# Global units' scores and values in the four accumulator banks at the start of a chunk

## The chip, the cores and the metric

One Trainium2 chip, one of its cores. The kernel is timed as a whole, in microseconds on the device; a figure for a kernel is the median of several runs. Five engines work side by side, each through its own queue in order: TensorE (PE; PEld is its weight load), VectorE (DVE), ScalarE (ACT), GpSimd (POOL) and SyncE (SP), which issues the DMA transfers. They wait for each other by semaphores.

## The reference

Attention with a window and a few global tokens, then a feed-forward layer with a norm ahead of it and a residual sum. Batch 8, 8 heads, 512 local and 32 global tokens, head dimension 64, so a model width of 512 and a hidden width of 2048.

```
s_g = scale * matmul(q_g, concat(k_g, k_l)^T)              # global queries see all 544 keys
out_g = matmul(softmax(s_g), concat(v_g, v_l))
s_ll = where(|i - j| <= 32, scale * matmul(q_l, k_l^T), -1e9)
out_l = matmul(softmax(concat(scale * matmul(q_l, k_g^T), s_ll)), concat(v_g, v_l))
x = concat(out_g, out_l) per token, heads side by side
out = x + relu((x - mean) / sqrt(var + 1e-6) * g_ln @ w_ch1) @ w_ch2
```

## The kernel before

**Chunks.** The local tokens are 16 halves of 256 tokens; two halves are a chunk of 512, chunks 0 to 7, and the 256 global tokens are the last, chunk 8. For each chunk `Ffn.run` goes through f = 0 to 15, 128 hidden units each. hidden(f) is 12 matmuls (line 777) into one of the two banks of `ps_h`. relu(f), on ScalarE, writes `hh` (line 788), rest(f), on VectorE, writes `hl` (line 792); both read that bank, and with rest(f) it comes free. out(f) is 4 times 3 matmuls (line 804) into the four accumulators `acc` of `ps_o`; the first of the three takes `hl`. On TensorE stand hidden(0), hidden(1), out(0), hidden(2), out(1) and so on. After out(15) line 836 adds the residual, held in tile `ob`, to each accumulator, and line 837 stores it. So the accumulators hold nothing from that sum to out(0) of the next chunk.

**What runs in between.** During chunk c the attention of chunk c+1 is made, piece by piece. `step()` is called three times in each hidden(f), once ahead of each of the four parts of out(f), and runs the next piece of a generator from the queue `first` or else `side`. At place 2f or 2f+1 (ahead of hidden(f) or behind it) `stage` adds generators to `side`. All engines' orders are as written (manual schedule).

A **pair** (`Pair`, four per chunk, places 1, 8, 16, 23) is two heads' pairs of a half: scores into two banks of `ps_a` (line 436), two reductions of four parts (line 454), exponentials (line 469), transposes by 32x32 blocks on VectorE (`turn_blocks`, line 395), values (line 504) into a bank of `ps_h`, sums on POOL, output (lines 521, 523). `attend(u, before, last)` runs pair u's scores, the earlier pair's values, half of u's reductions, the output of the earlier pair, the other half. Every second pair ends a half: its tokens are then normalized (lines 226 to 242, with a power on POOL between lines 228 and 236) and turned, also by line 395.

A **global unit** (`Global`, eight: one each in chunks 1 to 6, two in chunk 7) holds the 32 global queries of four batches and two heads. Its scores are 544 columns, made as two parts of 272, each into both banks of `ps_a`, from `ride` at places 3 and 6 through the queue `first`; reductions are line 582, exponentials line 595, transposes at places 11 and 16, values (line 627) at the end of the pair at place 23. `load`, called there for the next unit, asks for queries, keys and values together. The last two units run in chunk 7.

**Banks of `ps_h`.** A pair's values take the bank that is free when TensorE comes to them. For the pair at place 16, whose values stand between out(6) with hidden(7) behind it and hidden(8), that is the bank of f=6, and hidden(8) then takes the bank of f=7: it needs rest(7).

Of the kernel before, what the change touches and what calls it, by code (L numbers as in the profile page):

```python
# [83 lines left out]
def attention_ffn_kernel(  # L84
# [457 lines left out]
    class Global:  # L542


        def __init__(self, bg, hp):
            self.at = bg, hp
            self.next = None
            self.pt = None

        def load(self):  # L550
            ap = apool
            self.q = ap.tile([P, BG, SG], F32, name="gq", tag="gq")
            self.k = ap.tile([P, BG, SA], F32, name="gk", tag="gk")
            self.v = [wtmp.tile([P, BG, 2, P], F32, name="gv", tag="tmp", bufs=2) for _ in range(2)]
            self.vt = const.tile([P, P], F32, name="gvt", tag="band")
            nc.sync.dma_start(self.q, gq[self.at])
            nc.sync.dma_start(self.k, gk[self.at])
# [4 lines left out]
        def scores(self, part):  # L562
            if part == 0:
                self.p = apool.tile([P, 2, SA], F32, name="gp", tag="gp")
                self.mn = small.tile([P, 4], F32, name="gmn", tag="mn2")
                self.sm = small.tile([P, 2], F32, name="gsm", tag="sm2")
            p, mn = self.p, self.mn
            c0, c1 = part * SA // 2, (part + 1) * SA // 2
            sc = [ps_a.tile([P, 512], F32, name="sc", tag="att") for _ in range(2)]
            for i in range(BG):  # L570
                for h in range(2):
                    nc.tensor.matmul(  # L572
                        sc[h][i * SG:(i + 1) * SG, :c1 - c0],
                        self.q[h * D:(h + 1) * D, i, :],
                        self.k[h * D:(h + 1) * D, i, c0:c1],
                        start=True,
                        stop=True,
                        tile_position=(h * D, i * SG),
                        skip_group_check=True,
                    )  # L580
            for h in range(2):
                nc.vector.tensor_scalar(
                    p[:, h, c0:c1],
                    sc[h][:, :c1 - c0],
                    -QSCALE,
                    BIG if part == 0 else mn[:, 2 * h:2 * h + 1],
                    ALU.mult,
                    ALU.min,
                    accum_out=mn[:, 2 * h + part:2 * h + part + 1],
                )  # L590
            yield
            if part == 0:
                return
            for h in range(2):
                nc.scalar.activation(
                    p[:, h, :],
                    p[:, h, :],
                    AF.Exp,
                    bias=mn[:, 2 * h + 1:2 * h + 2],
                    scale=-1.0,  # L600
                    accum_out=self.sm[:, h:h + 1],
                )
                yield

        def turned(self):
            if self.pt is None:
                pt = apool.tile([P, 2, SA], F32, name="gpt", tag="gk")
                self.pt = pt[:, :, :4 * P].rearrange("p h (c q) -> p h c q", c=4)
                self.tail = pt[:, :, 4 * P:]
# [9 lines left out]

        def values(self):  # L620
            bg, hp = self.at
            pv = ps_a.tile([P, 512], F32, name="pv", tag="att")
            for h, c in [(h, c) for h in range(2) for c in range(4)] + [(0, 4), (1, 4)]:
                hd = slice(h * D, (h + 1) * D)
                for i in range(BG):
# [9 lines left out]
                    )  # L635
            ri = small.tile([P, 2], F32, name="gri", tag="ri2")
            nc.gpsimd.tensor_scalar(ri, self.sm, SUM_EPS, None, ALU.add)
            yield
            nc.vector.reciprocal(ri, ri)
            x = apool.tile([P, P], F32, name="gx", tag="gq")  # L640
            nc.vector.tensor_tensor(
                x.rearrange("p (h d) -> p h d", h=2),
                pv[:, :P].rearrange("p (h d) -> p h d", h=2),
                ri.unsqueeze(2).to_broadcast([P, 2, D]),
                op=ALU.mult,
            )
            to = xs.rearrange("(b s) d -> b s d", b=B)[bg * BG:(bg + 1) * BG, :SG]
            nc.sync.dma_start(to[:, :, hp * P:(hp + 1) * P], x)
            if self.next:
                self.next.load()  # L650
            yield

# [225 lines left out]

    def attend(u, before, last):

        if u:
            u.scores()
            if u.next:
                u.next.load_scores()
        if before:
            before.values()
            before.sums()
            if before.next:
                before.next.load_values()
# [36 lines left out]
        for n in range(4 if u else 0):  # L926
            u.turn(4 + n)
            yield

    xt = []  # L930
# [105 lines left out]
    for token in pend:  # L1036
        firsts.does(token)
    side.append(finish_first())
    new = list(zip(pairs[5:] + [None], pairs[4:]))
    for c, chunk in enumerate(chunks):  # L1040
        if c == 1:
            globals_[0].load()
        if chunk is None:
# [10 lines left out]

        def ride(u, places):
            for n, place in enumerate(places[:2]):
                put(place, lambda n=n: first.append(u.scores(n)) or ())
            for n, place in enumerate(places[2:]):
                put(place, lambda n=n: u.turns(n))

        if 0 < c < last_chunk - 1:
            for place in PAIR_PLACES:
                u, before = new.pop(0)
                last = globals_[c - 1].values if place == PAIR_PLACES[-1] else None
                put(place, lambda u=u, before=before, last=last: attend(u, before, last))
            ride(globals_[c - 1], (3, 6, 11, 16))
        if c == last_chunk - 1:
            ready[last_chunk] = [new_x()]
            x = ready[last_chunk][0]
            put(2, lambda: load_global_tokens(0))  # L1070
            ride(globals_[c - 1], (1, 4, 6, 8))
            put(11, globals_[c - 1].values)
            ride(globals_[c], (14, 16, 17, 18))
            put(21, globals_[c].values)
            put(22, lambda: load_global_tokens(1))
# [109 lines left out]
```

## Time and profile before

| | |
|---|---|
| median of 3 runs (lowest, highest) | 908.58 us (907.88, 909.33) |
| span of the profiled execution | 904.6 us |
| TensorE busy | 886.3 us (98%) |
| VectorE busy | 647.9 us (72%) |
| ScalarE busy | 306.6 us (34%) |
| GpSimd busy | 36.2 us (4%) |
| mean granted TensorE clock | 0.994 |

A row of time gives start, length, engine, line of the program, operation, tile written and read, shape, count of instructions merged into it; in brackets stands the idle time of the engine before it and who ended it. A matmul of 32-bit floats that is not rounded (line 436, 504, 572, 627) leaves two records. Records of matmuls overlap, since they are pipelined: the start of the next tells more than an end.

### The profile page before, as it was taken

The numbers are of one execution on the slowest core, as the hardware profiler recorded it, in microseconds if no ns is written. First come the engines' busy times: TensorE is split into PE (matmuls) and PEld (weight loads), VectorE is DVE, ScalarE is ACT, GpSimd is POOL, SyncE is SP. The second block draws the span as 40 slices with busy tenths as digits, with TensorE's granted clock in tenths as the row PEclk, the third lists the DMA queues.
The fourth block names the chain that finished last, engine by engine and source line by source line (L and its number), as shares of the span: only waits on it lengthen the run. The fifth ranks groups of instructions, "written<-read, shape, count | busy, mean of one in ns | idle before, by whom it ended". The sixth has DMA issues, their size and how long they took to land.

```text
span 904.6 us, 20622 instructions
## 1 busy us (share of the span) xinstructions
PE 886.3 (98%) x8492; PEld 703.4 (78%) x8492; DVE 647.9 (72%) x1818; ACT 306.6 (34%) x849; POOL 36.2 (4%) x107
## 2 busy tenths in 40 slices
PE   5899999999999999999999999999999999999998
PEld 3788778778778777778777777788777777777897
DVE  7999945787868877787868877787877863433611
ACT  7877844323232223322223223322223212111211
POOL 2100110000000000000000000000000000000000
PEclk9899999999999999999999999999999999999999
DMA  9993355422433246322433246222533142031100
GB/s 358 415 416 114 125 174 192 147 76 95 161 125 102 78 156 218 105 74 87 170 125 102 79 150 224 85 91 74 186 125 102 47 165 70 1 105 62 47 24 23
DMA packets 48110, 119.29 MB, mean 132 GB/s; under 512 B 4240, under 2 KB 15504, under 8 KB 44944
## 3 DMA queue, kind: packets, MB, share of 16 engines
q1 hardware_dynamic: 48016, 117.98, 37.1%
q8 instruction: 66, 1.08, 0.5%
q14 instruction: 28, 0.23, 0.1%
HBM read 100.14 MB, written 17.83 MB: 130 GB/s over the span
## 4 chain that ended last, share of the span: by engine, by line
PE 94%; DVE 2%; DMA 1%; ACT 1%; issue 0%; POOL 0%; SPq 0%; DVEq 0%
PE ph L777 42%; PE acc L804 42%; PE sc L436 3%; PE pv L504 3%; PE sc L572 1%; PE pv L627 1%; DMA gk<-in_gk 1%; DMA raw<-in_wd 1%; PE t L677 1%; DVE tmp L195 0%; PE tp L484 0%; DVE p L321 0%; ACT p L335 0%; PE sc L304 0%; DMA xs<-gx 0%
## 5 line engine op out<-in xcount | busy, mean ns | idle before, releaser
L804 PE MATMUL acc<-w,hh 128*128 128x512 f32 x1088 | 342.0, 395 | 0.0
L777 PE MATMUL ph<-xh,w 128*128 128x512 f32 (+1 forms) x1240 | 310.2, 376 | 0.0
L777 PEld LDWEIGHTS ph<-xh,w 128*128 128x128 f32 x1240 | 217.1, 188 | 49.4 <-issue 3.3
L804 PEld LDWEIGHTS acc<-w,hh 128*128 128x128 f32 x1088 | 204.9, 188 | 47.6
L788 ACT ACTIVATE hh<-ph 128x512 fp32r<-128x512 f32 (+1 forms) x147 | 82.9, 564 | 451.0 <-PE ph L777 449.9
L792 DVE SCALAR_TENSOR_TENSOR hl<-ph,hh 128x512 fp32r<-128x512 f32 (+1 forms) x147 | 95.7, 651 | 171.0 <-ACT hh L788 169.5
L804 PE MATMUL acc<-w,hl 128*128 128x512 f32 x544 | 218.0, 401 | 0.0
L395 DVE STREAM_TRANSPOSE pt<-p 32x256 f32<-32x256 f32 x368 | 160.3, 436 | 11.9 <-ACT p L469 6.5
L777 PE MATMUL ph<-xl,w 128*128 128x512 f32 (+1 forms) x524 | 141.9, 392 | 0.0
L804 PEld LDWEIGHTS acc<-w,hl 128*128 128x128 f32 x544 | 102.1, 188 | 24.1 <-issue 0.4
L777 PEld LDWEIGHTS ph<-xl,w 128*128 128x128 f32 x524 | 96.5, 188 | 26.2 <-issue 3.9
L469 ACT ACTIVATE p<-p,mn 128x128 f32<-128x128 f32 x224 | 87.3, 392 | 66.0 <-DVE mn L454 64.7
L395 DVE STREAM_TRANSPOSE x<-x 32x256 f32<-32x256 f32 x208 | 90.6, 436 | 5.4 <-ACT x L242 2.5
L454 DVE CUSTOM_DVE_ANT_0 p<-sc,mask 128x128 f32<-128x128 f32 x224 | 51.4, 288 | 18.6 <-PE sc L436 18.4
L395 DVE STREAM_TRANSPOSE gpt<-gp 32x256 f32<-32x256 f32 x128 | 55.5, 433 | 2.0
L469 ACT ACTIVATION_READ_ACCUMULATOR p<-p,mn 128x1 f32 x224 | 42.1, 188 | 0.0
L436 PEld LDWEIGHTS sc<-e 64*32 64x32 f32 x1792 | 25.3, 107 | 10.0 <-issue 9.8
L436 PE MATMUL sc<-e 64*32 64x128 f32 x1792 | 32.8, 276 | 0.0
L504 PEld LDWEIGHTS pv<-v,pt 128*32 128x32 f32 x1792 | 26.3, 110 | 6.0 <-issue 5.2
L504 PE MATMUL pv<-v,pt 128*32 128x64 f32 x1792 | 30.8, 220 | 0.0
L242 ACT ACTIVATE x<-x,rs 128x512 f32<-128x512 f32 x30 | 22.8, 809 | 22.3 <-DVE rs L236 22.3
L516 POOL TENSOR_SCALAR ri<-sm 128x8 f32<-128x8 f32 x29 | 9.5, 327 | 411.5 <-ACT p L469 410.5
(76 smaller groups left out, 486.4 us busy)
## 6 DMA issues: line engine op xcount, KB each, us to landing
v<-in_eu SPq DMA_DIRECT2D x28, 1024.0 KB, 7.4
e<-in_eu SPq DMA_DIRECT2D x28, 672.0 KB, 4.0
raw<-in_wd SPq DMA_DIRECT2D x16, 1024.0 KB, 12.9
ob<-xs SPq DMA_DIRECT2D x34, 256.0 KB, 6.7
out<-ob SPq DMA_DIRECT2D x34, 256.0 KB, 2.6
gk<-in_gk SPq DMA_DIRECT2D x8, 1088.0 KB, 5.4
xs<-x SPq DMA_DIRECT2D x32, 256.0 KB, 7.6
gv<-in_gv SPq DMA_DIRECT2D x16, 512.0 KB, 6.5
```

The costliest lines, as they stand in the source:

```text
L242: nc.scalar.activation(self.xn[:, j, :], self.x[:, j, :], AF.Identity, bias=self.rs[:, 1, j:j + 1], scale=self.rs[:, 0, j:j + 1],)
L395: nc.vector.transpose(out=to[rp][..., gp], in_=a[gp][..., rp])
L436: nc.tensor.matmul(sc[h][gp, at:at + P], self.e[hd, j, w * WIN:(w + 1) * WIN], self.e[hd, j, k0 * WIN:(k0 + 4) * WIN], start=True, stop=Tr ...
L454: nc.vector.tensor_tensor_reduce(out=self.p[:, j, c], in0=self.sc[h][:, at:at + P], in1=masks[self.at[2], qb], scale=-QSCALE, scalar=BIG, ...
L469: nc.scalar.activation(self.p[:, j, c], self.p[:, j, c], AF.Exp, bias=self.mn[:, j, c:c + 1], scale=-1.0, accum_out=self.sm[:, j, c:c + 1],)
L504: nc.tensor.matmul(self.pv[gp, at:at + D], self.pt[:, j, 2 * h + qb, gp], self.v[:, j, 4 * qb + g, h * D:(h + 1) * D], start=True, stop=Tr ...
L516: nc.gpsimd.tensor_scalar(self.ri, self.sm, SUM_EPS, None, ALU.add)
L572: nc.tensor.matmul(sc[h][i * SG:(i + 1) * SG, :c1 - c0], self.q[h * D:(h + 1) * D, i, :], self.k[h * D:(h + 1) * D, i, c0:c1], start=True, ...
L777: nc.tensor.matmul(ph[:, :n], w[:, kt, :], xx[kt][:, part.start:part.start + n], start=(i == 0), stop=(i == 3 * KT - 1),)
L788: nc.scalar.activation(hh[:, :n], self.ph[f, start][:, :n], AF.Relu)
L792: nc.vector.scalar_tensor_tensor(hl[:, :n], self.ph[f, start][:, :n], 0.0, f32(hh[:, :n]), ALU.max, ALU.subtract)
L804: nc.tensor.matmul(self.acc[t], a[:, ts], w, start=(f == 0 and i == 0), stop=(f == NF - 1 and i == 2),)
```

## The change

The keys of a unit are split 512 and 32 instead of 272 and 272. In chunks 1 to 6 the first `attend` of a chunk also makes the global unit's scores, the 512 columns of two heads in the first two accumulators and the 32 columns in the other two, and, in columns 128 to 256 of the last of them, the values of the unit before. The reductions of the unit, the output of the unit before and the loads come in the same piece. The pair's own reductions now come in the next two pieces, in every `attend`, both behind the output of the earlier pair; the unit's exponentials follow the pair's. `gp` moves to the tag of the residual tile `ob`, `gpt` to that of `gp`. Keys and queries are loaded one unit ahead; values when the values before are done. In chunk 7 the seventh unit's scores and the sixth's values are at place 1, and the rest of the last two at place 9 in `end_global`.

```diff
-        def load(self):
...
+        def load_scores(self):
...
+        def load_values(self):
+            self.v = [wtmp.tile([P, BG, 2, P], F32, name="gv", tag="tmp", bufs=2) for _ in range(2)]
...
+        def keys(self, part):
+            return ((0, 4 * P), (4 * P, SA))[part]
+
+        def scores(self, part, banks):
+            self.banks[part] = banks
+            c0, c1 = self.keys(part)
...
+        def reduce(self, part):
+            if part == 0:
+                self.p = fpool.tile([P, 2, SA], F32, name="gp", tag="ob")
...
-        def values(self):
-            pv = ps_a.tile([P, 512], F32, name="pv", tag="att")
+        def values(self, pv):
+            self.pv = pv
...
-    def attend(u, before, last):
+    def accumulators():
+        return [ps_o.tile([P, 512], F32, name="gsc", tag=f"acc{t}") for t in range(4)]
+
+    def attend(u, before, g=None, g_before=None):
         if u:
             u.scores()
             if u.next:
                 u.next.load_scores()
+        if g:
+            banks = accumulators()
+            g.scores(0, banks[:2])
+            g.scores(1, banks[2:])
         if before:
             before.values()
             before.sums()
             if before.next:
                 before.next.load_values()
-        if u:
-            u.reduce(0)
-            u.exps(0)
+        if g_before:
+            g_before.values(banks[3][:, P:2 * P])
+        if g:
+            g.reduce(0)
+            g.reduce(1)
+            if g_before:
+                g_before.output()
+            g.load_values()
+            if g.next:
+                g.next.load_scores()
         if before:
             before.output()
         yield
         if u:
+            u.reduce(0)
+            u.exps(0)
+            yield
+        if u:
             u.reduce(1)
             u.exps(1)
             yield
+        if g:
+            for h in range(2):
+                g.exps(h)
+                yield
...
-        if last:
-            yield from last()
...
+    def end_global(before, g):
+        g.scores(0, [ps_a.tile([P, 512], F32, name="sc", tag="att") for _ in range(2)])
+        before.values(ps_h.tile([P, 512], F32, name="pv", tag="ph")[:, :P])
+        before.output("pt2")
+        g.load_values()
+        g.reduce(0)
+        for n in range(14):
+            yield
+        g.scores(1, [ps_a.tile([P, 512], F32, name="sc", tag="att") for _ in range(2)])
+        g.reduce(1)
...
-            ride(globals_[c - 1], (3, 6, 11, 16))
+                if place == PAIR_PLACES[0]:
+                    us += globals_[c - 1], globals_[c - 2] if c > 1 else None
+            for n in range(2):
+                put((11, 16)[n], lambda n=n, c=c: globals_[c - 1].turns(n))
         if c == last_chunk - 1:
+            put(1, lambda: attend(None, None, *globals_[c - 1:c - 3:-1]))
+            put(9, lambda: end_global(*globals_[c - 1:]))
```

Lines of the program shift: 582 becomes 589, 792 becomes 796, 627 becomes 634. In the orders below `ISA` is one masked reduction of a pair, followed each time by a row that reads its accumulator (left out); `hl` is rest(f).

VectorE at the start of chunk 2, from rest(0) to rest(2), before:

```order
L792 SCALAR_TENSOR_TENSOR hl<-ph,hh 128x512
L454 ISA p_3186,mn_3185<-sc,mask_96 128x128
...
L521 RECIPROCAL ri_3181<-ri_3181 128x8
L523 TENSOR_TENSOR x<-pv,ri_3181 128x2x128 x2
...
L395 STREAM_TRANSPOSE pt_3209<-p_3186 32x8x32 x6
L792 SCALAR_TENSOR_TENSOR hl<-ph,hh 128x512
L395 STREAM_TRANSPOSE pt_3209<-p_3186 32x8x32 x10
L582 TENSOR_SCALAR gp,gmn<-sc 128x272 x2
L792 SCALAR_TENSOR_TENSOR hl<-ph,hh 128x512
```

The same place after:

```order
L796 SCALAR_TENSOR_TENSOR hl<-ph,hh 128x512
L589 TENSOR_SCALAR gp,gmn<-gsc 128x512 x2
L589 TENSOR_SCALAR gp,gmn<-gsc,gmn 128x32 x2
L646 RECIPROCAL gsm<-gsm 128x2
L648 TENSOR_TENSOR gx<-gsc,gsm 128x128
L521 RECIPROCAL ri_3149<-ri_3149 128x8
L523 TENSOR_TENSOR x<-pv,ri_3149 128x2x128 x2
L454 ISA p_3218,mn_3217<-sc,mask_96 128x128
...
L796 SCALAR_TENSOR_TENSOR hl<-ph,hh 128x512
L395 STREAM_TRANSPOSE pt_3257<-p_3218 32x8x32 x14
L796 SCALAR_TENSOR_TENSOR hl<-ph,hh 128x512
```

All eight reductions of the pair stand behind the global unit's work and the output, and fourteen block transposes, not six and ten, between two writes of `hl`.

VectorE from the pair at place 8 of the same chunk to rest(7), before, from the last reduction on:

```order
L454 ISA p_3420,mn_3419<-sc,mask_122 128x128
...
L226 BN_STATS st<-x 128x6 x2
L228 BN_AGGR mv<-st 128x2 x2
L792 SCALAR_TENSOR_TENSOR hl<-ph,hh 128x512
L236 SCALAR_TENSOR_TENSOR rs<-mv,rs 128x2
L395 STREAM_TRANSPOSE pt_3478<-p_3420 32x8x32 x8
L395 STREAM_TRANSPOSE x<-x 32x8x32 x2
...
L395 STREAM_TRANSPOSE x<-x 32x8x32 x14
...
L395 STREAM_TRANSPOSE gpt<-gp 32x2x4x32 x6
```

The same place after, from the output on:

```order
L523 TENSOR_TENSOR x<-pv,ri_3418 128x2x128 x2
L454 ISA p_3430,mn_3429<-sc,mask_114 128x128
...
L796 SCALAR_TENSOR_TENSOR hl<-ph,hh 128x512
L226 BN_STATS st<-x 128x6 x2
L228 BN_AGGR mv<-st 128x2 x2
L236 SCALAR_TENSOR_TENSOR rs<-mv,rs 128x2
L395 STREAM_TRANSPOSE pt_3484<-p_3430 32x8x32 x8
...
L395 STREAM_TRANSPOSE x<-x 32x8x32 x14
...
L395 STREAM_TRANSPOSE gpt<-gp 32x2x4x32 x4
```

The norm's statistics moved behind rest(4), and the shift that waits for POOL has no write of `hl` ahead of it any more; each half of the transposes begins a little later against the writes of `hl`.

TensorE at the start of chunk 2, after:

```order
L436 MATMUL sc<-e 32x128 x32
L572 MATMUL gsc<-gk,gq 32x512 x8
L572 MATMUL gsc<-gk,gq 32x32 x8
L504 MATMUL pv<-v,pt_2857 32x64 x32
L634 MATMUL gsc<-gv,gpt 32x64 x32
L634 MATMUL gsc<-gvt,gpt 32x64 x8
```

Before, the first and the fourth stood there alone; the others stood as two groups of `32x272 x8` inside hidden matmuls and one group of values between two parts of out(f).

## Rows read from the trace of the kernel before

**Rows 1.** Busy time in one chunk: stretch, length, PE, PEld, DVE, ACT, POOL, PEclk, DMA

```profile
354.10:456.20 102.10, 102.10 (x1009) 80.49 (x1008) 80.86 (x237) 30.37 (x96) 3.06 (x9) 1.00 0.36 123
```

**Rows 2.** TensorE's global groups in time, chunk 3; then two groups by line

```profile
361.89 1.10 PE L777 MATMUL ph<-xh,w 128*128 128x512 f32 x4
...
363.86 0.69 PE L572 MATMUL sc<-gk,gq 64*32 64x272 f32 x16
...
365.52 0.40 PE L804 MATMUL acc<-w,hl 128*128 128x512 f32 x1
...
430.80 1.10 PE L627 MATMUL pv<-gv,gpt 128*32 128x64 f32 x64
...
432.19 0.51 PE L804 MATMUL acc<-w,hl 128*128 128x512 f32 x1
...
L436 PE MATMUL sc<-e 64*32 64x128 f32 x1792 | 32.8, 276 | 0.0
...
L572 PE MATMUL sc<-gk,gq 64*32 64x272 f32 x256 | 11.0, 401 | 0.2 <-DMA gk<-in_gk 0.2
```

**Rows 3.** TensorE in time from place 8 to hidden(8), chunk 3

```profile
376.96 1.20 PE L777 MATMUL ph<-xh,w 128*128 128x512 f32 x4
...
393.86 1.10 PE L777 MATMUL ph<-xh,w 128*128 128x512 f32 x4
...
396.67 0.40 PE L804 MATMUL acc<-w,hl 128*128 128x512 f32 x1
...
401.69 1.20 PE L777 MATMUL ph<-xh,w 128*128 128x512 f32 x4
```

**Rows 4.** VectorE in time over the same stretch

```profile
376.03 0.29 DVE L454 CUSTOM_DVE_ANT_0 p<-sc,mask 128x128 f32<-128x128 f32 x1 [2.51 <-PE sc L436]
...
377.19 0.76 DVE L523 TENSOR_TENSOR x<-pv,ri 128x256 f32<-128x256 f32 x2
...
377.86 0.28 DVE L454 CUSTOM_DVE_ANT_0 p<-sc,mask 128x128 f32<-128x128 f32 x1
...
378.70 1.28 DVE L226 BATCH_NORM_STATS2 st<-x 128x6 f32<-128x512 f32 x2
...
380.75 0.69 DVE L792 SCALAR_TENSOR_TENSOR hl<-ph,hh 128x512 fp32r<-128x512 f32 x1 [0.55 <-ACT hh L788]
...
381.42 3.57 DVE L395 STREAM_TRANSPOSE pt<-p 32x256 f32<-32x256 f32 x8
...
387.07 6.29 DVE L395 STREAM_TRANSPOSE x<-x 32x256 f32<-32x256 f32 x14
393.39 0.69 DVE L792 SCALAR_TENSOR_TENSOR hl<-ph,hh 128x512 fp32r<-128x512 f32 x1
...
400.58 0.69 DVE L792 SCALAR_TENSOR_TENSOR hl<-ph,hh 128x512 fp32r<-128x512 f32 x1
```

**Rows 5.** VectorE in time at place 23 of chunk 6

```profile
731.49 0.30 DVE L228 BATCH_NORM_AGGREGATE mv<-st 128x2 f32<-128x6 f32 x2
732.93 0.16 DVE L236 SCALAR_TENSOR_TENSOR rs<-mv,rs 128x2 f32<-128x2 f32 x1 [1.14 <-POOL rs L233]
...
733.51 0.29 DVE L641 TENSOR_TENSOR gx<-pv,gri 128x128 f32<-128x128 f32 x1
```

**Rows 6.** ScalarE in time, chunk 3

```profile
372.69 0.74 ACT L595 ACTIVATE gp<-gp,gmn 128x544 f32<-128x544 f32 x1
...
376.43 0.40 ACT L469 ACTIVATE p<-p,mn 128x128 f32<-128x128 f32 x1 [2.90 <-DVE mn L454]
...
380.12 0.60 ACT L788 ACTIVATE hh<-ph 128x512 fp32r<-128x512 f32 x1 [0.28 <-PE ph L777]
```

**Rows 7.** DMA issues of the page: count, KB each, us from issue to landing

```profile
out<-ob SPq DMA_DIRECT2D x34, 256.0 KB, 2.6
```

**Rows 8.** Busy time and clock in two stretches of chunk 0, columns as rows 1

```profile
30.70:34.10 3.40, 1.43 (x45) 1.07 (x38) 3.37 (x16) 3.15 (x11) 1.11 (x4) 1.00 1.05 420
34.20:37.50 3.30, 3.30 (x50) 2.97 (x56) 3.14 (x7) 2.49 (x6) 0.08 (x1) 0.50 1.04 436
```

More of the change, by code (lines that the diff above doesn't have):

```diff
@@ L580, in scores, with exps @@
                     )
+        def reduce(self, part):
+            if part == 0:
+                self.p = fpool.tile([P, 2, SA], F32, name="gp", tag="ob")
+                self.mn = small.tile([P, 4], F32, name="gmn", tag="mn2")
+            c0, c1 = self.keys(part)
             for h in range(2):
+                c = 2 * h + part
                 nc.vector.tensor_scalar(
[L583 to L584 removed]
+                    self.p[:, h, c0:c1],
+                    self.banks[part][h][:, :c1 - c0],
                     -QSCALE,
[L586 removed]
+                    self.mn[:, c - 1:c] if part else BIG,
                     ALU.mult,
                     ALU.min,
[L589 removed]
+                    accum_out=self.mn[:, c:c + 1],
                 )
[L591 to L603, printed above, removed]
+        def exps(self, h):
+            if h == 0:
+                self.sm = small.tile([P, 2], F32, name="gsm", bufs=2)
+            nc.scalar.activation(
+                self.p[:, h, :],
+                self.p[:, h, :],
+                AF.Exp,
+                bias=self.mn[:, 2 * h + 1:2 * h + 2],
+                scale=-1.0,
+                accum_out=self.sm[:, h:h + 1],
+            )
+            if h == 1:
+                nc.gpsimd.tensor_scalar(self.sm, self.sm, SUM_EPS, None, ALU.add)
         def turned(self):
             if self.pt is None:
[L607 removed]
+                pt = apool.tile([P, 2, SA], F32, name="gpt", tag="gp")
                 self.pt = pt[:, :, :4 * P].rearrange("p h (c q) -> p h c q", c=4)
@@ L635, in values, with output @@
                     )
[L636 to L640, printed above, removed]
+        def output(self, tag="gq"):
+            bg, hp = self.at
+            nc.vector.reciprocal(self.sm, self.sm)
+            x = apool.tile([P, P], F32, name="gx", tag=tag)
             nc.vector.tensor_tensor(
                 x.rearrange("p (h d) -> p h d", h=2),
-                pv[:, :P].rearrange("p (h d) -> p h d", h=2),
-                ri.unsqueeze(2).to_broadcast([P, 2, D]),
+                self.pv.rearrange("p (h d) -> p h d", h=2),
+                self.sm.unsqueeze(2).to_broadcast([P, 2, D]),
                 op=ALU.mult,
@@ L928, in attend @@
             yield
+    def end_global(before, g):
[8 more added lines that the diff above has]
+        g.reduce(1)
+        yield
+        for h in range(2):
+            g.exps(h)
+            yield
+        for n in range(2):
+            yield from g.turns(n)
+        for n in range(14):
+            yield
+        g.values(ps_a.tile([P, 512], F32, name="pv", tag="att")[:, :P])
+        g.output()
+        yield
     xt = []
@@ L1053, in put @@
             at.setdefault(place, []).append(run)
[L1055 to L1059, printed above, removed]
         if 0 < c < last_chunk - 1:
             for place in PAIR_PLACES:
-                u, before = new.pop(0)
-                last = globals_[c - 1].values if place == PAIR_PLACES[-1] else None
-                put(place, lambda u=u, before=before, last=last: attend(u, before, last))
-            ride(globals_[c - 1], (3, 6, 11, 16))
+                us = new.pop(0)
+                if place == PAIR_PLACES[0]:
+                    us += globals_[c - 1], globals_[c - 2] if c > 1 else None
+                put(place, lambda us=us: attend(*us))
+            for n in range(2):
+                put((11, 16)[n], lambda n=n, c=c: globals_[c - 1].turns(n))
         if c == last_chunk - 1:
```

33 lines of the change are left out of this document (9 added, 24 removed).

## The prediction

> **What bounds the kernel now.** Begin with the busy shares in the table: TensorE 98%, the next engine 72%. One middle chunk says it more sharply: 102.10 us of TensorE in 102.10 us, at granted clock 1.00, VectorE 80.86, ScalarE 30.36 [rows 1]. So nothing hides behind TensorE; each microsecond that it gains or waits is one of the result. Next come its rows inside a chunk, for the price of the global unit: the three groups that the change moves each stand alone among full-width matmuls [rows 2]. Last, the rows of VectorE beside TensorE's between two pairs [rows 3, 4]: TensorE waits for nothing there, but how much room is left? The write of `hl` for f=7 starts at 400.58 and lasts 0.69, to 401.27. hidden(8) starts at 401.69. As the bank that hidden(8) writes is the one which that write reads, the room is 0.42 us. This is the place to watch, because the change moves VectorE's order ahead of it.
>
> The profiled execution spans 904.6 us; the median is 908.6, so about 4.0 us lie around the span, and I leave them as they are.
>
> **What is saved on TensorE.** Twelve hidden matmuls take 2.81 (393.86 to 396.67) [rows 3]. With a scores group of 16 records among them they take 361.89 to 365.52, 3.63: a group costs 0.82, of which its own records are 0.69 or, by the start of what follows, about 0.62, and some 0.2 is the change of tile in and out. The values group fills 430.80 to 432.19, 1.39, and with the same 0.2 costs 1.59 [rows 2]. A unit is two scores groups and one values group, 3.23; eight units are 25.8, and the last waits some 0.3 for its late keys (0.2 and its surroundings: the only wait for `gk` in the row of line 572): 26.1.
>
> After: 512 and 32 columns stand in place of two times 272. Records of 272 columns last 401 ns and those of 128 last 276 [rows 2], 0.87 ns per column; a scores group is two records deep, so 240 more columns add 0.4 to 0.62, 1.0. What 32 columns cost no row shows. They cannot be under nothing, since the same sixteen records must be issued, and not over the 0.62 of records eight times as long; the nearest row is the pair's (128 columns, 17 ns from record to record), 0.27. In the pair's block fill and change of tile are shared; I take 1.2 for both parts and 1.36 for values. Six blocks with scores, 7.2; five of them with values, 6.8; in chunk 7 four groups alone: scores with values 2.8, scores with values 2.6, the 32 columns 0.5, values 1.6, 7.5 in all. Sum 21.5. **Saved: 4.6 us** (3.5 to 6, by the ends of the 32-column part and of the fill). This is the only saving.
>
> **What VectorE's new order costs: the place after f=7.** In `attend`, the pair's reductions now stand behind the output of the pair before, which needs the values; half of them stood ahead of it. I count from V, the start of full matmuls after the values (376.96).
>
> Output starts V+0.23 and passes on 0.67 later (377.19, 377.86) [rows 4], V+0.90. All eight reductions follow, 0.84 for four (377.86 to 378.70), to V+2.58. The first exponential follows a first reduction by 0.40 (376.03, and 376.43 in the next group), V+1.30; eight at 0.39 and the last accumulator read, 3.2, to V+4.5. relu(4) is queued behind them on ScalarE; it was ready at 380.12, V+3.16. It takes 0.60 [rows 6], to V+5.1, and rest(4), the write of `hl`, 0.61, to V+5.7. Norm statistics, ahead of rest(4) until now and partly in its shadow, come behind it: 1.28, V+7.0. Aggregate to shift is 1.44, most of it VectorE waiting for POOL (731.49, 732.93) [rows 5]; before, rest(4) stood in that gap. V+8.4. Then nothing idles any more: eight transposes 3.6 (381.42), rest(5) 0.7, fourteen transposes 6.32 (387.07 to 393.39), rest(6) begins at V+19.1. From rest(6) to rest(7) 7.19 (393.39 to 400.58); the new order has the same fifteen transposes there. rest(7) begins at V+26.3 and ends at **V+27.0**. hidden(8) wants its bank at 401.69, V+24.73. **TensorE waits 2.25 us**, in each of chunks 1 to 6: 13.5. The 0.55 us for which VectorE was idle before rest(4) [rows 4] is used up, and no other slack is left to absorb it.
>
> **The same at the start of a chunk.** There the new block has global work too. With V again the end of all values: the last bank's 32-column reduction waits for the values written to that bank, V+0.23, and takes some 0.2; reciprocal and `gx` 0.5 (733.51) [rows 5], reciprocal and output of the pair 1.0, V+1.9. Exponentials from V+2.3 to V+5.5; then two of the global unit, 0.75 each (372.69) [rows 6], V+7.0; relu(1) V+7.6; rest(1) V+8.3; fourteen transposes 6.32, V+14.6; rest(2) ends at V+15.3. out(2) begins with that `hl`: hidden(1), out(0), hidden(2), out(1), hidden(3) are five stages of 2.8 and 0.1 for the change of tile, V+14.1. **Wait 1.2**; in chunk 1, without earlier values and `gx`, some 0.4 of it less, 0.85. Five times 1.2 and 0.9: 6.9. After it rest(3) has a free f, and VectorE idles before place 8; the two waits don't add into each other.
>
> **Edits at nothing.** Scores into accumulators: the last residual sum must have read them; hidden(0) and the pair's scores, 2.9 and 1.1 us, lie between. The scores' tile `gp` takes the residual buffer, whose stores land 2.6 us after their issue [rows 7]; with the global scores 5 us lie between the last accumulation and the first reduction, and what exceeds them has some 0.7 more before it shows, since VectorE waits for the values anyway. out(0) needs its bank only 2.9 after V, reductions end near V+0.4. Keys are asked for a chunk early: this covers the 0.3 counted above. Moving value loads behind the values leaves them a whole chunk. The sum on POOL follows the exponentials and has most of a chunk.
>
> **Sum.** 13.5 + 6.9 − 4.6 = +15.8. Span 904.6 + 15.8 = 920.4, with 4.0 around it **924.4 us**.
>
> **Rivals.**
> 1. *Faster: VectorE keeps its room.* The two waits vanish if rest(7) ends before V+24.73 and rest(2) before V+14.1, that is if the delays are 2.25 and 1.2 shorter than summed. Then only the saving is left: 908.6 − 4.6 = 904.0. For it: TensorE waits nowhere in chunk 3, and VectorE has 21 us free per chunk [rows 1]. Against it: that free time lies elsewhere; from 387.07 fourteen transposes run straight into rest(6) at 393.39, and the 7.19 to rest(7) are its work without a pause [rows 4]. 8 in 100.
> 2. *No change: only the chunk start costs.* If the norm's gap shrinks, say because POOL is done early as before, and relu(4) finds ScalarE free, place 16 has its 0.42 back: 908.6 + 6.9 − 4.6 = 910.9 down to 907 when the start too is half of what I sum. 6 in 100.
> 3. *Slower still: TensorE's clock.* A wait of 2 us has a precedent: in 30.70 to 34.10 TensorE was busy for 1.43 of 3.40 us, and the next stretch, 34.20 to 37.50, shows 0.50, the 1.2 GHz level [rows 8]. If each of the six longer waits is followed by such a stretch, 3.3 us at half speed costs 1.65, six make 9.9: 934. Against it: the work around the waits here is dense full-width matmuls, there it was small tiles. 14 in 100, of which most would be some of the six, not all.
> [...]
> 4. *It does not do what it says:* were an accumulator still held, scores would wait for it. With 2 us of room after the last residual sum I give this 2 in 100; each us of it costs six.
>
> **How the numbers follow.** Forecast 924.4, 70 in 100, and its own ends: waits of 1.8 to 2.6 and 0.7 to 1.5, saving 3.5 to 6: 908.6 + 15 − 6 = 917.6 to 908.6 + 24.6 − 3.5 = 929.7. A range of 8 in 10 has to leave out rival 1, rival 2's half and the far end of rival 3: 914 to 932. A change of 0.2%, 1.8 us, is about what a measurement of this kernel can tell. Faster by more: rival 1, 8 in 100. Within: most of rival 2, 5. Slower: 87.
>
> **What would show it.** Right: chunk period about 105 us in place of 102.1; in each of chunks 1 to 6 one gap of TensorE before hidden(8), ended by VectorE's `hl`, of some 2.2 us, and one of about 1.2 before out(2); VectorE without idle time from the norm's shift to hidden(8); the 512-column group at about 1.0 us, no groups of scores or values alone before chunk 7; no gap before the last unit's scores. Wrong: VectorE idle shortly before f=7's `hl`, or a gap that DMA ends (residual stores, rival 4), or PEclk under 1.00 in the middle (rival 3). The forecast fails first at the two ends on VectorE, V+27.0 and V+15.3: each 0.1 us there is 0.6 us of the result.

## The result, and the profile after

| | before | after |
|---|---|---|
| median (lowest, highest), us | 908.44 (907.88, 909.33) | 921.14 (920.44, 923.34) |
| span of the profiled execution, us | 904.6 | 919.4 |
| mean granted TensorE clock | 0.994 | 0.995 |

The changed kernel is slower: ratio 1.0144, 95% interval 1.0122 to 1.0165. The median lies 3.3 us under the forecast of 924.4 and inside its range. The profiled execution of after took 921.18 us, 1.8 more than its span.

The page's busy line, then what TensorE waited for from 140 to 860 us (waiter, releaser: total us, times, longest):

```profile
PE 882.8 (96%) x8492; PEld 706.2 (77%) x8492; DVE 646.0 (70%) x1818; ACT 301.5 (33%) x849; POOL 37.2 (4%) x107
```

```profile
PE ph L781 <- DVE hl L796: 9.5, 6, 1.6
PE gsc L634 <- issue: 4.4, 3, 2.5
PE acc L808 <- DVE hl L796: 2.3, 5, 0.5
```

TensorE is busy 3.5 us less than before (886.3) and waits in three places. The first is hidden(8), the third out(2), as forecast. The second was not forecast: a stop inside the moved values, for which the trace names no semaphore ("issue").

Chunks 2 to 5, each from its first pair's scores to the next chunk's, with the columns of [rows 1]:

```profile
252.06:356.63 104.57, 101.98 (x1009) 81.17 (x1008) 80.68 (x237) 29.48 (x96) 3.06 (x9) 1.00 0.36 121
356.63:461.90 105.27, 101.77 (x1010) 81.12 (x1009) 80.67 (x237) 29.48 (x96) 3.06 (x9) 1.00 0.36 119
461.90:569.22 107.32, 103.25 (x1010) 82.39 (x1009) 80.65 (x237) 29.47 (x96) 3.06 (x9) 0.98 0.36 118
569.22:672.98 103.76, 101.77 (x1010) 81.02 (x1009) 80.65 (x237) 29.48 (x96) 3.06 (x9) 1.00 0.37 120
```

All were 102.1 long before [rows 1]. They now differ among themselves, which two waits of fixed length cannot explain.

**hidden(8) and out(2).** TensorE in time, chunk 3: hidden(3) and out(2), then pair scores, pair values and hidden(8). This answers [rows 3].

```profile
373.74 1.10 PE L781 MATMUL ph<-xh,w 128*128 128x512 f32 x4
...
377.19 0.50 PE L808 MATMUL acc<-w,hl 128*128 128x512 f32 x1 [0.48 <-DVE hl L796]
...
404.92 1.16 PE L436 MATMUL sc<-e 64*32 64x128 f32 x64
406.00 1.34 PE L504 MATMUL pv<-v,pt 128*32 128x64 f32 x64
408.93 0.96 PE L781 MATMUL ph<-xh,w 128*128 128x512 f32 x3 [1.58 <-DVE hl L796]
```

From the start of the values to hidden(8) it is 2.92 us, where before it was 1.03 (400.66 to the 401.69 of [rows 3]): 1.89 of waiting. From hidden(3) to out(2) it is 3.44 against 2.80: 0.64. (The bracket counts from a modelled end, so it is smaller.)

VectorE over the stretch that [rows 4] showed, from the pair's output to rest(7), V being 382.30:

```profile
382.44 0.76 DVE L523 TENSOR_TENSOR x<-pv,ri 128x256 f32<-128x256 f32 x2 [3.55 <-PE pv L504]
383.11 0.28 DVE L454 CUSTOM_DVE_ANT_0 p<-sc,mask 128x128 f32<-128x128 f32 x1
...
387.14 0.69 DVE L796 SCALAR_TENSOR_TENSOR hl<-ph,hh 128x512 fp32r<-128x512 f32 x1 [2.27 <-ACT hh L792]
387.75 1.28 DVE L226 BATCH_NORM_STATS2 st<-x 128x6 f32<-128x512 f32 x2
388.94 0.30 DVE L228 BATCH_NORM_AGGREGATE mv<-st 128x2 f32<-128x6 f32 x2
390.38 0.16 DVE L236 SCALAR_TENSOR_TENSOR rs<-mv,rs 128x2 f32<-128x2 f32 x1 [1.14 <-POOL rs L233]
390.46 3.57 DVE L395 STREAM_TRANSPOSE pt<-p 32x256 f32<-32x256 f32 x8
...
400.97 0.69 DVE L796 SCALAR_TENSOR_TENSOR hl<-ph,hh 128x512 fp32r<-128x512 f32 x1
...
408.18 0.69 DVE L796 SCALAR_TENSOR_TENSOR hl<-ph,hh 128x512 fp32r<-128x512 f32 x1
```

The statistics stand behind rest(4) in the open, the gap for POOL is empty (1.14), and from 390.46 nothing idles. rest(7) ends at 408.87, and hidden(8) starts 0.06 later.

**The stops.** TensorE in time: the end of the block in chunk 5, where it runs through, and in chunk 4:

```profile
571.22 1.10 PE L504 MATMUL pv<-v,pt 128*32 128x64 f32 x64
572.14 1.08 PE L634 MATMUL gsc<-gv,gpt 128*32 128x64 f32 x64
573.15 0.43 PE L634 MATMUL gsc<-gvt,gpt 32*32 32x64 f32 x16
573.50 0.73 PE L781 MATMUL ph<-xh,w 128*128 128x512 f32 x2
```

```profile
464.82 1.08 PE L634 MATMUL gsc<-gv,gpt 128*32 128x64 f32 x64
465.83 0.41 PE L634 MATMUL gsc<-gvt,gpt 32*32 32x64 f32 x13
468.73 0.30 PE L634 MATMUL gsc<-gvt,gpt 32*32 32x64 f32 x3 [2.49 <-issue]
468.95 1.20 PE L781 MATMUL ph<-xh,w 128*128 128x512 f32 x4
469.99 1.78 PE L781 MATMUL ph<-xl,w 128*128 128x512 f32 x4
471.57 1.91 PE L781 MATMUL ph<-xh,w 128*128 128x512 f32 x4
473.27 0.53 PE L808 MATMUL acc<-w,hl 128*128 128x512 f32 x1
```

In chunk 4 thirteen of sixteen matmuls of one group run, then nothing for 2.70 us (start to start), then the last three. The same happens for 0.74 us in chunk 2, behind the 51st record of the group before, and for 1.66 us in chunk 3, between the two groups; not in chunks 1, 5 and 6. Behind the long stop the hidden matmuls take up to 0.43 us each (1.70 for the last four) in place of 0.23: hidden(1) lasts 4.32, and should last 2.90. The granted clock there:

```profile
470.20:473.27 3.07, 3.07 (x8) 2.34 (x7) 2.10 (x18) 2.41 (x13) 0.00 (x0) 0.50 0.55 154
```

A count of the records gave the first clue. Each matmul record has a weight load, so the block is 240 records and 480 instructions. Counted from the first instruction of TensorE in the trace, the three stops come behind number 5569, 7616 and 9665: 193, 192 and 193 modulo 256 (the rest that a division by 256 leaves). The page lists a DMA queue that brings instructions, in packets of 16 KB (count, MB, share):

```profile
q8 instruction: 66, 1.08, 0.5%
```

66 packets for 17,064 instructions are some 259 instructions a packet, and the stops lie 2047 and 2049 apart, eight times 256: a packet is 256 instructions. The trace has the packets in time:

| chunk | stop begins (last start) | packet on its way | TensorE goes on | end of packet to going on |
|---|---|---|---|---|
| 2 | 255.71 | 254.07 to 255.11 | 256.45 | 1.34 |
| 3 | 360.41 | 358.88 to 360.55 | 362.07 | 1.52 |
| 4 | 466.03 | 466.48 to 467.46 | 468.73 | 1.27 |

So the theory to test, theory S: TensorE has run out of instructions. If the stops mark where a packet is needed, no packet of this trace starts more than 297 instructions ahead of that, and 16 of the 66 start between 290 and 297 ahead. At the earliest a packet thus starts when TensorE is some 300 instructions short of needing it; with a full-width matmul every 0.23 us it then has 35 us. The block goes through 300 instructions in under 3 us.

### The profile page after: what moved, and what is told of

Read it like the earlier page. It is cut to its first block, busy times and chain, and to the rows that moved or that the text cites. A ratio compares the mean times of both kernels' runs of the same rounds, so it can differ in the third digit from the quotient of the medians.

```text
span 919.4 us, 20601 instructions
## 1 busy us (share of the span) xinstructions
PE 882.8 (96%) x8492; PEld 706.2 (77%) x8492; DVE 646.0 (70%) x1818; ACT 301.5 (33%) x849; POOL 37.2 (4%) x107
## 4 chain that ended last, share of the span: by engine, by line
PE 71%; DVE 20%; ACT 5%; issue 2%; POOL 1%; DMA 1%; ACTq 0%; DVEq 0%
PE acc L808 31%; PE ph L781 30%; DVE pt L395 8%; DVE x L395 4%; ACT p L469 4%; PE sc L436 3%; DVE hl L796 3%; PE pv L504 2%; DVE gpt L395 1%; PE gsc L634 1%; DVE x L523 1%; ACT gp L602 1%; DVE st L226 1%; PE gsc L572 1%; ACT hh L792 1%
## 5 line engine op out<-in xcount | busy, mean ns | idle before, releaser
L523 DVE TENSOR_TENSOR x<-pv,ri 128x256 f32<-128x256 f32 x56 | 21.1, 419 | 27.7 <-PE pv L504 26.5
```

The source lines that it names most:

```text
L523: nc.vector.tensor_tensor(x[:, :, (hp + j) * P:(hp + j + 1) * P].rearrange("p q (h d) -> p q h d", h=2), self.pv[:, j * 256:(j + 1) * 256] ...
```

## The experiments

Each edit is of the kernel after, unless it says otherwise. "Before" beside each is a set of runs on the same chip; its median was 907.0 to 909.1.

**What makes hidden(8) wait?** The change made two edits to the pair's part of `attend`: the first half of the reductions went behind the output of the earlier pair, and a piece boundary was added ahead of it. Each is undone alone.

```diff
         if u:
             u.reduce(0)
             u.exps(0)
-            yield
+            if g:
+                yield
```

> The kernel after, without the extra piece boundary: at places 8, 16 and 23 both halves of the pair's reductions and exponentials go into one piece again, still behind the earlier pair's output. So the norm's statistics come one piece earlier, ahead of rest(4). Theory: of the delay that makes hidden(8) wait 1.89 us, some 2.5 us come from these statistics standing behind rest(4) in the open (statistics, aggregate and POOL's power to 390.46, where rest(4) could lie in their shadow). Then rest(7) ends some 2.5 us earlier, the wait of 1.8 us (records 1801 ns apart) before hidden(8) is gone in all of chunks 1 to 6, 6 x 1.89 = 11.3, 921.1 - 11.3 = about 910. Rival: the order alone (reductions behind the output, exponentials 0.9 us and more later) makes the wait; then at least 1 us of it stays in each chunk and the time is 915 or more. The waits before out(2) and the stops inside the block at a chunk's start stay as they are.

Measured: 912.55 us (912.24 to 913.86). TensorE's waits, then VectorE from the statistics to rest(7), chunk 3:

```profile
PE ph L781 <- DVE hl L796: 1.2, 6, 0.2
```

```profile
382.36 1.28 DVE L226 BATCH_NORM_STATS2 st<-x 128x6 f32<-128x512 f32 x2
...
384.70 0.69 DVE L796 SCALAR_TENSOR_TENSOR hl<-ph,hh 128x512 fp32r<-128x512 f32 x1 [0.85 <-ACT hh L792]
385.31 0.15 DVE L236 SCALAR_TENSOR_TENSOR rs<-mv,rs 128x2 f32<-128x2 f32 x1
...
404.12 0.69 DVE L796 SCALAR_TENSOR_TENSOR hl<-ph,hh 128x512 fp32r<-128x512 f32 x1
```

The statistics lie in the shadow of ScalarE again and rest(4) in that of POOL. Of the wait of 1.6 (by this view) 0.2 is left; from start to start 0.26 of 1.89. The transposes begin 2.6 us earlier in relation to V, but rest(7) comes only 1.6 earlier, since with one piece less two more transposes (0.9 us) stand ahead of rest(5). In six chunks what is left is 1.6 of the 2.6 us over the 910 expected. Where the other 1.0 comes from is not shown for the median; in the profiled execution, the longest of the five (913.86), chunk 4's stop was 3.13 us and hidden(1) behind it lasted 5.29, and hidden(1) of chunk 5 had a stop of 0.67 between two matmuls.

```diff
+        if u and not g:
+            u.reduce(0)
+            u.exps(0)
         if before:
             before.output()
         yield
         if u:
-            u.reduce(0)
-            u.exps(0)
+            if g:
+                u.reduce(0)
+                u.exps(0)
             yield
```

> The kernel after, with the other half of the edit undone: at places 8, 16 and 23 the first half of the reductions and exponentials stands ahead of the earlier pair's output again; the extra piece boundary stays, so the norm's statistics stay behind rest(4). Theory (statistics behind rest(4) are the larger part): exponentials start some 1.7 us earlier, but relu(4) cannot start before hidden(4) is done, 3.2 us behind the values, so only some 1.1 us of the 1.89 come back; about 0.8 us of wait before hidden(8) stays in each of chunks 1 to 6: 921.1 - 6.5 = 914.6. Rival (the order alone makes the wait): it vanishes, 910.

Measured: 914.87 us (914.25 to 916.05).

```profile
PE ph L781 <- DVE hl L796: 4.7, 6, 0.8
```

0.8 of the 1.6 is left; from start to start 0.84 of 1.89. So the boundary is the larger part: undoing it brings back 1.63, undoing the order 1.05. The rival, in which the order alone makes the wait, falls in both.

To see whether the boundary does it without any move of global work, it was put into the kernel before:

```diff
         if before:
             before.output()
         yield
         if u:
+            yield
             u.reduce(1)
```

> The kernel before, with one line: in attend an empty piece between the output and the second half of the reductions, in every pair. Nothing global is moved. Theory (the norm's statistics slip behind rest(4)): TensorE waits for rest(7) before hidden(8) as in the kernel whose reductions were put ahead again, about 1.0 us in each of chunks 1 to 6: 908.5 + 6 = 914.5. Rival: that wait came from the move of the unit's work and the order before has room for a piece more: 908.5.

Measured: 911.84 us (911.22 to 915.49), 1.0043 (1.0026 to 1.0061) times before; span 909.6, 5.0 over the profile of before.

```profile
PE ph L777 <- DVE hl L792: 4.6, 6, 0.8
```

The same wait as in e2, 0.84 from start to start, in a kernel with nothing else changed: one empty piece costs 0.4%. That is 3.5 us by the medians and 5.0 by the two profiled executions, where 6 were expected. Before, rest(7) ended at V+24.31 (401.27 less 376.96). It ends at V+25.52 in e8, with the boundary alone, at V+24.95 in e1, with the order alone, and at V+26.57 in after, with both: 1.2, 0.6 and 2.3 us later.

**What makes out(2) wait?**

```diff
-        if g:
-            for h in range(2):
-                g.exps(h)
-                yield
+        if g:
+            for h in range(2):
+                yield
...
+        if g:
+            for h in range(2):
+                g.exps(h)
         for n in range(4 if u else 0):
             u.turn(n)
```

> The kernel after, with one move: at a chunk's start the two exponentials of the global unit (ACT, 0.73 and a read of 0.18 each, 1.47 together) come three pieces later, behind relu(1) instead of ahead of it. Theory: they hold relu(1) up, from there rest(1), fourteen transposes and rest(2), whose hl out(2) takes 0.64 us late in chunks 1, 2, 3, 5 and 6. With relu(1) 1.47 earlier that wait is gone in all five: 921.1 - 3.2 = 918. Rival: it is the order on VectorE (the unit's reductions and both outputs ahead of the pair's reductions) that makes it; then at least 0.3 us of it stays. The wait before hidden(8), 1.89 in six chunks, and the stops in the values group stay.

Measured: 919.23 us (917.86 to 919.80). The view has no row for out(2) any more: the wait is gone in all five chunks. ScalarE, chunk 3, after and e5: relu(1) behind and ahead of the unit's exponentials.

```profile
367.46 0.74 ACT L602 ACTIVATE gp<-gp,gmn 128x544 f32<-128x544 f32 x1
...
368.93 0.57 ACT L792 ACTIVATE hh<-ph 128x512 fp32r<-128x512 f32 x1
```

```profile
366.94 0.58 ACT L792 ACTIVATE hh<-ph 128x512 fp32r<-128x512 f32 x1
367.42 0.74 ACT L602 ACTIVATE gp<-gp,gmn 128x544 f32<-128x544 f32 x1
```

Stops of 0.65, 1.27 and 2.98 us stayed in chunks 2, 3 and 4, and so did the half-speed matmuls behind the last. A fourth stop came that after did not have, in hidden(1) of chunk 5, right behind the block: 0.91 us between two matmuls that are 0.23 apart otherwise, again at 193 modulo 256.

```profile
PE ph L781 <- issue: 0.5, 1, 0.5
```

**What stops the values?** Two theories: the supply of instructions as such (S), or the loads of `e` and `v` that are issued while the block runs (D).

```diff
             u.scores()
-            if u.next:
+            if u.next and not g:
                 u.next.load_scores()
...
-            if before.next:
+            if before.next and not g:
                 before.next.load_values()
...
             g.load_values()
+            if u:
+                if u.next:
+                    u.next.load_scores()
+                if before.next:
+                    before.next.load_values()
```

> The kernel after, at place 1 alone with the loads of the next pair's keys and values (e and v) moved behind the load of gv in SyncE's order, which waits for the global values: no load is issued while the block of scores and values runs. TensorE's instructions and their order are unchanged. In the kernel after TensorE stops inside the global values, with no semaphore to wait for, for 0.74, 1.66 and 2.70 us (start to start) in chunks 2, 3 and 4. Theory S (supply of instructions: the three stops are at the same count of records modulo 256, and a fetch of 16 KB on the instruction queue ends 1.3 to 1.5 us before each end of a stop): with quiet DMA the fetch takes some 3.5 us from its trigger, and stops of about 0.7, 0.6 and 1.2 us stay in chunks 2, 3 and 4; 921.1 - 2.6, with the seven half-speed matmuls of chunk 4 gone too (1.4), 917 to 919. Theory D (the loads hold the fetch or the operands up): all three stops are gone, 921.1 - 6.4 = 914.7. A theory that neither bears on it: stops unchanged, 921.

Measured: 919.02 us (917.46 to 920.93).

```profile
PE gsc L634 <- issue: 2.6, 3, 0.9
```

Stops of 1.00, 1.07 and 1.14 us stay, behind the same three instructions, and chunk 4 has no half-speed matmuls. With quiet queues it takes 3.5 to 3.9 us from 300 instructions ahead of the stop until TensorE goes on; with the loads, in the kernel after, it took 3.6, 4.5 and 5.0. D alone is out. Of chunk 4's 2.70 the loads made some 1.6. Since chunk 4 was no longer late there, out(2) waited in it too, 0.6.

```diff
+    def more():
+        ts = [ps_a.tile([P, 512], F32, name="sc", tag="att") for _ in range(2)]
+        for n in range(44):
+            h, s = n % 2, n // 2 % 4
+            nc.tensor.matmul(ts[h][s * WIN:(s + 1) * WIN, :P], ...)
+        yield
...
+            if c == 1:
+                put(13, more)
```

> The kernel after, with 44 small matmuls (88 records, with their weight loads 176 instructions) added once, in chunk 1 at place 13, into banks that nobody reads; they cost some 1.5 us themselves. All later instructions of TensorE stand 176 further; everything else in the blocks is unchanged, the loads too. Theory S (a stop comes where the count of instructions reaches 193 modulo 256 inside the block, if the fetch for it was triggered, some 301 instructions earlier, after the block began): the stops leave chunks 2 and 3 and come in chunks 5 and 6, 0.7 to 2.2 us each; chunk 4 has one of 0 to 2. Time 918 to 925. Theory D (loads alone): the stops stay in chunks 2, 3 and 4 with about 0.7, 1.7 and 2.7 us, none in 5 and 6; 922.6.

Measured: 917.63 us (916.85 to 919.44). TensorE in time around the block of chunks 5 and 6:

```profile
566.48 0.28 PE L634 MATMUL gsc<-gv,gpt 128*32 128x64 f32 x2
567.32 0.88 PE L634 MATMUL gsc<-gv,gpt 128*32 128x64 f32 x48 [0.56 <-issue]
```

```profile
671.18 0.40 PE L634 MATMUL gsc<-gv,gpt 128*32 128x64 f32 x15
672.26 0.91 PE L634 MATMUL gsc<-gv,gpt 128*32 128x64 f32 x49 [0.68 <-issue]
```

The stops left chunks 2 and 3 and came in 5 and 6, 0.78 and 0.90 us, again at 193 modulo 256. Chunk 4 keeps a short one at the same count, now earlier in the block, in the pair's values: 0.50 us between two matmuls.

```profile
PE pv L504 <- issue: 0.3, 1, 0.3
```

The loads were as in the kernel after. A kernel with 88 matmul records more is 3.5 us faster, because 176 instructions shift where its packets end; the records themselves cost little, since hidden(8) of chunk 1 waits right behind them anyway (0.2 in place of 1.6). D would have left the stops where they were; S said where they would go.

```diff
-        if g_before:
-            g_before.values(banks[3][:, P:2 * P])
...
         else:
+            for n in range(1 if u else 4):
+                yield
+            if g:
+                if g_before:
+                    g_before.values(banks[3][:, P:2 * P])
+                    g_before.output()
+                g.load_values()
...
             yield
```

> The kernel after, with the values of the unit before taken out of the block: they stand in hidden(1), behind 8 of its 12 matmuls (in chunk 7 behind hidden(1)), and the output and the loads of gv, gq and gk go with them. The block is 160 records, 320 instructions, in place of 240 and 480. Theory S (supply of instructions; 301 of them between trigger and need, 3.5 to 5 us to bring 256): no stop in the block or in the values in any chunk, and no half-speed matmuls, -6.4. The values alone cost some 0.2 us more each, +1. As the exponentials no longer wait for the global values but out(2) does, the wait before out(2) goes in chunks 2, 3, 5 and 6 too, -2.5, and stays at 0.64 in chunk 1. 921.1 - 6.4 + 1 - 2.5 = 913.2. Rival: a stop of some 1 us stays in the chunks 2 to 4, if already 320 instructions are too many; 916.

Measured: 915.50 us (914.79 to 915.53).

```profile
PE gsc L634 <- issue: 1.1, 1, 1.1
```

There is no stop in the shorter block, and out(2) waits in chunk 1 alone, although the unit's exponentials still stand ahead of relu(1): the chain on VectorE and ScalarE now starts before the global values are done. One stop of 1.31 us is left in the values of chunk 4, where the packet was due during the loads: 5.7 us passed from the point 300 instructions ahead until TensorE went on. So the 8 hidden matmuls between were not enough there; the stop is 1.3 of the 2.3 us by which the time exceeds the 913.2 expected.

**All repairs together.** The pair's order and pieces as before the change, the values in hidden(1), the unit's exponentials behind relu(1):

```diff
+        if u and not g:
+            u.reduce(0)
+            u.exps(0)
         if before:
             before.output()
         yield
-        if u:
+        if u and g:
             u.reduce(0)
             u.exps(0)
             yield
```

> The kernel after with three repairs: at places 8, 16 and 23 the reductions and pieces as in the kernel before (both halves of the edit undone); the values of the unit before in hidden(1); the unit's exponentials behind relu(1). Theory: all waits and stops that the change brought are gone, and what the change saves on TensorE is left: 921.1 - 11.3 (hidden(8)) - 3.2 (out(2)) - 6.4 (stops and half-speed matmuls) + 1 (values alone) = 901.2, some 7 us under the kernel before. Rival: what was saved was only the 4.6 of the prediction less 1 for the split: 905. If a wait comes back elsewhere, 909 or more.

Measured: 902.95 us (902.46 to 903.15), 0.9944 (0.9926 to 0.9962) times before.

```profile
PE gsc L634 <- issue: 0.6, 1, 0.6
```

The last stop, chunk 4's, is left; it is half of the 1.7 us over the 901.2 expected. It goes with the loads behind the values, as in e3:

```diff
                 g.load_values()
+                if u:
+                    u.next.load_scores()
+                    before.next.load_values()
```

> The kernel e7_all_three, with the loads of e and v at place 1 behind the load of gv in SyncE's order, as in e3. In e7 one stop is left, 0.85 us in the values of chunk 4, 5.3 us behind the point where the fetch for it is triggered, with e and v under way; and a hidden matmul of chunk 5 comes 0.2 late. Theory: the loads alone lengthen that fetch from some 3.5 us to 5.3; with quiet queues there is no stop in any chunk, TensorE stands nowhere over 0.3 us between chunks 1 and 6, and the time is 902.95 - 1.3 = 901.6, inside what the measurement can tell from no change; the trace decides. Rival: the fetch takes as long without the loads, and the stop stays at 0.5 us or more.

Measured: 902.17 us (901.84 to 902.94), 0.9946 (0.9933 to 0.9960) times before. The view of TensorE's waits from 140 to 860 us is empty. Chunks 3 and 4:

```profile
351.52:452.95 101.43, 101.43 (x1009) 80.97 (x1008) 80.72 (x237) 30.02 (x96) 3.04 (x9) 1.00 0.36 124
452.95:554.38 101.43, 101.43 (x1010) 80.97 (x1009) 80.73 (x237) 30.02 (x96) 3.04 (x9) 1.00 0.36 124
```

0.7 us a chunk under [rows 1]: that is what moving the unit's scores into the block, with its values in hidden(1), saves once nothing waits for it. This kernel and e7 are some 0.5% faster than the kernel before, clear of noise, and 2% faster than the kernel after; from each other they differ by less than the measurement tells, but the trace shows the stop gone.

## Why the prediction was right, and where it was not

The sum by steps, span against span (904.6 to 919.4, +14.8):

| step | predicted | measured |
|---|---|---|
| hidden(8) waits for rest(7), six chunks | 6 x 2.25 = 13.5 | 6 x 1.89 = 11.3 |
| out(2) waits for rest(2) | 5 x 1.2 + 0.9 = 6.9 | 4 x 0.64 + 0.57 = 3.1 |
| saved on TensorE | 4.6 | 6.0 |
| stops in the values | none | 0.8 + 1.5 + 2.8 = 5.1 |
| half-speed matmuls behind the stop of chunk 4 | rival 3 | 1.4 |
| sum | +15.8 | +14.9 |
| around the span | 4.0 | 1.8 |

The stops here are the lengthening of the stretch in which they lie. "Saved" is what is left of each chunk's length with its waits taken off: 2.2 in chunk 1, which lost a unit's values to the next, 0.8 to 0.9 in each of chunks 2 to 5, 0.3 in all that follows; 6.0 in sum.

**hidden(8): right in place, cause and sign; mis-sized by 0.36.** The chain ran as summed, each link somewhat shorter: the reductions begin at V+0.81 (0.90 summed), rest(4) at V+4.84 (5.1), the transposes at V+8.16 (8.4), rest(6) at V+18.67 (19.1), rest(7) ends at V+26.57 (27.0). Links that were each taken a little long add up to 0.4 us over a chain of 26. e1, e2 and e8 show the cause: mostly the piece boundary, which the prediction had as "norm statistics ... come behind it".

**out(2): right in place and cause, twice too large.** Again each link was taken a little long: exponentials begin at V+1.93 (2.3), relu(1) at V+6.5 (7.0), rest(2) ends at V+14.7 (15.3). The wait is the small difference of two long paths, so 0.6 of error is half of it. Chunk 4 had no such wait, since the slow matmuls made TensorE late. Chunk 1 waited as long as the others, not less: with no global values ahead of it, V comes there while the unit's reductions still run (151.63 to 153.24, V at 152.61), and the exponentials begin at V+1.92 all the same. That the chain over VectorE and ScalarE makes the wait is shown twice: e5 takes the unit's exponentials out of it, e6 the global values from its start, and either is enough. So ScalarE's order is a cause of it and not the only one.

**The saving: 1.4 too small.** The unit's scores were summed at 1.2 with the 32 columns and took 1.11; the values 1.36, as summed (572.14 to 573.50). What was missed is the pair's own part: its scores and values take 0.90 and 0.92 in the block, where they take 1.09 and 1.03 alone. In the block each is followed by a group of the unit with the same tile (64*32, then 128*32), so a change of tile is spared. That is 0.30 a chunk, 1.8 in six, more than the 1.4; which other term was taken too low is open.

**The stops: not foreseen, the failed step.** "I take 1.2 for both parts and 1.36 for values" priced the block by its rows and asked for banks, buffers and loads, but not whether TensorE could be fed so long a run of small matmuls. Before, the longest such run was a pair's 128 records, 256 instructions, and it never stopped: the trace of before could not show the limit. It did show the queue and the size of its packets. The Trainium skill (Runtime: NRT & Kernel Launch, "Instruction fetch mechanics") says that instructions are refilled in blocks of 16 KiB, 256 instructions, and that crossing a block's edge is mostly hidden. On the block the trace agrees: 66 packets of 16 KB. On the hiding it does not where matmuls are this small: in eight kernels (after, e1 to e7) all 19 stops inside a global group, and the three beside one (e1, e4, e5), came at 192 or 193 modulo 256, and TensorE went on 1.2 to 1.5 us after the packet's end.

**Rival 3, the clock, came true once.** The waits of 1.9 us, 29 in the five kernels that have them at full length, left the clock at 1.00, as the prediction had it for most likely. The stops decided: behind 2.70 us (after), 3.13 (e1), 3.08 (e2) and 2.98 (e5) TensorE fell to the 1.2 GHz level for a stretch; behind stops up to 1.66 it did not. The Trainium skill (TensorE: Matmul & The Clock Gate, "Why this matters for your kernels") warns that long idle gaps between bursts of matmuls bring the lower level back, and means gaps longer than the six waits. The four longest stops agree, the shortest of them, 2.70, being a little under the length that the page names.

**Rivals 1, 2 and 4 did not occur**, and no gap stands before the last unit's scores. The repairs bring 902.2, a little under the 904.0 of rival 1, in which only the saving is left.

**Around the span.** 4.0 us was the difference of a median and the span of another execution, which was one of the shorter ones; executions of the kernel before ranged from 905.7 to 911.3 us over all sets. In after, time less span is 1.8 in each execution. That the median came out within 3.3 us owes something to errors of both signs: +2.2, +3.8 and +2.2 too much for the waits and the surroundings, 1.4 too little saved, and 6.5 left out. So the places and causes of the two waits were right by reasoning, and the closeness of the total was in part luck.

## What to carry to other kernels

Work moved onto an engine that is full is judged by the order it forces on the others: a piece boundary that puts a step of a long chain out of another's shadow costs more than the moved matmuls save. When a wait is the difference of two long paths, give it a wide range, and undo each half of an edit alone. And count instructions in a run of small matmuls: a run longer than those the trace already shows to go through is a cost of its own, to be split by full-width matmuls and kept clear of loads (eight alone were not enough in e6, eight with quiet queues were in e9).

## What the hardware showed that was not expected

TensorE can run dry of instructions. Its packets of 256 come one ahead: about 300 instructions lie between the point from which a packet is fetched and the point where it is needed, worked out from the packets' starts, and from the first point until TensorE goes on it takes 3.5 to 3.9 us with quiet DMA queues (e3) and up to 5.7 with loads under way (e6). Runs of 480 small instructions in 4.3 us stopped for 0.65 to 3.13 us wherever both points fell into the run, and for 0.50 where the first lay at its very start (e4); which chunk that was could be shifted by 176 instructions ahead of it (e4). In the longest stops it is the packet's start that comes late: 2.8 to 3.3 us behind the first point (chunk 4 of after, e1, e2, e5, e6 and e7), against 1.1 to 1.4 in e3 and e4; the packet itself takes 0.9 to 1.7 in all of them. Whether the packet is late because of the queue it shares or of memory was not tried.
